# Attention and a SwiGLU block in one kernel: key rests of four heads in one score unit, a written-out order for batch 0, loads ordered by need

## The chip, the cores and the metric

The kernel runs on one core of a Trainium2 chip. The metric is the device time of one execution, in microseconds. Before the change the median of three runs is 453.41 us (453.38 to 453.52). The profile is of one execution whose instructions span 451.7 us.

In the profile PE is TensorE (PEld its weight loads), ACT is ScalarE, DVE is VectorE, POOL is GpSimd and SP is SyncE, which here only issues DMA. A "chunk" or "unit" in this text is one PSUM tile of scores with the one exponential that reads it.

## What is computed

Eight batches of twelve heads, 448 positions, head size 64. Softmax attention, heads put side by side into rows of 768, then a gated FFN with 1536 inner columns:

```python
scores = q @ k.T / sqrt(64)                 # per batch and head, 448 x 448
attn   = softmax(scores)                    # over keys
x      = (attn @ v) -> [8*448, 768]         # heads side by side
g      = x @ w_gate                         # [3584, 1536]
out    = (g * sigmoid(g) * (x @ w_val)) @ w_out     # [3584, 768], float32
```

## The kernel before

Matmuls run in FP16 with FP32 accumulation. Two heads make a pair: 48 pairs, six per batch. Scores are computed transposed, keys on partitions, so that the exponentials can be the stationary operand of the product with V. A column of ones beside V gives the sum of the exponentials, and the division comes at the end, on 128 queries at a time.

The 448 keys of a pair are cut into four chunks of 112. A chunk is two matmuls (one for each head, on the upper and the lower 64 rows of the array) and one exponential over 896 columns:

```python
def qk(pr, c):
    t = qkT[pr]
    s = ps_s.tile([128, 2, 512], FP32, tag="s")          # ring of 3, two banks each
    for hx in range(2):
        nc.tensor.matmul(s[:, hx, 0:S],
            lhsT=t[ts(hx, 64), c * P : c * P + 128],     # P = 112 keys
            rhs=t[ts(hx, 64), ds(S + (1 - hx) * D, S)], start=True, stop=True)
    e = Es[pr % NE][:, ds(c * EB, 16)].rearrange("p (h b) x -> p h (b x)", h=2)
    nc.scalar.activation(e[:, :, 0:S], s[0:P, :, 0:S], AF.Exp, scale=sm_scale)
```

The product with V (PV) takes 448 queries as three groups of 128 for each head; the remaining 64 queries of both heads share a seventh group, so that one accumulator of one PSUM bank holds a pair:

```python
def pv_chunk(pr, c):
    if c == 0:
        accs[pr] = ps_f.tile([128, 512], FP32, tag="f", name="acc")   # ring of 2 banks
    ...
    for j in range(3):
        for hx in range(2):
            nc.tensor.matmul(a7[:, 2 * j + hx], lhsT=e[...], rhs=vo[:, hx, c, 0 : D + 1], ...)
    for hx in range(2):
        nc.tensor.matmul(a7[:, 6], lhsT=e[...], rhs=vo[:, hx, c, 0 : D + 1], ...)
    ...                                # after the last chunk: reciprocal, multiply, into xt
```

That makes 8 matmuls of 65 columns a chunk and 32 a pair. The result must be turned (`turn_x`) to be the moving operand of the FFN. For pairs below XPE = 12 PE does it, with the rests of a batch turned together in `turn_rests`; from there on two DMA transposes do it. q and k are turned by PE below pair NPE = 11 (18 transposes of 112 columns a pair) and by DMA after that.

The FFN works in eight blocks of 384 and 512 tokens by turns. Each has 12 steps of gate and value (six matmuls each), and two output groups of 12 matmuls for each 128 tokens:

```python
gp = ps_f.tile(...) if gate_small[0] else ps_s.tile([128, 2, 512], FP32, tag="s")[:, 0]
group("g", gp)                                  # 6 matmuls
nc.scalar.activation(sg, gp, AF.Tanh, scale=0.5)
vp = ps_f.tile([128, 512], FP32, tag="f")
group("v", vp)                                  # 6 matmuls
... t = (sg + 1) * gp ; hts = t * vp            # both on DVE
```

The output of a chunk of 128 tokens is written at the end of its second half. The very last chunk is treated apart: its halves go out singly, and the second half in two pieces of 192 columns.

```python
last = last_block and ch == n // 128 - 1
...
parts = [(oh * OH, OH)]
if last and oh:
    parts = [(OH, OH // 2), (OH + OH // 2, OH // 2)]
```

The program has a start, in which the attention of batch 0 (pairs 0 to 5) is done as a loop over 24 chunks with PV, transposes and loads placed between them, and a main loop of "visits". A visit issues two or three chunks of scores, up to two PVs of earlier pairs, and a share of the FFN's steps. Loads are issued by GpSimd, which also turns FP32 into FP16 in the DMA; the lists `wq` say at which pair each load is issued.

Of the kernel before, what the change touches and what calls it, by code (L numbers as in the profile page):

```python
# [10 lines left out]
FP32 = mybir.dt.float32  # L11
# [6 lines left out]
NB = 2  # L18
GP = 3
NPE = 11  # L20
# [3 lines left out]
WIDE = 8  # L24
XPE = 12
NE = 4
NX = 6
NV = 5
VS = 9
EB = 15  # L30
# [3 lines left out]
def kernel(  # L34
# [24 lines left out]
    MQ = S - D  # L59
# [13 lines left out]
    load_table("exp_and_others")  # L73

# [7 lines left out]
    ps_f = ctx.enter_context(tc.tile_pool(name="ps_f", bufs=2, space=PSUM))  # L82

    Es = [consts.tile([P, NC * EB + 1, D], FP16, name=f"E{i}") for i in range(NE)]
    Xts = [consts.tile([128, 7, D], FP16, name=f"xt{i}") for i in range(NX)]
    Xrs = [consts.tile([D, 128], FP16, name=f"xr{i}") for i in range(3)]
    Vts = [consts.tile([P, 2, NC, D + 2], FP16, name=f"vo{i}") for i in range(NV)]
    vraw = consts.tile([P, VS, 2, NC, D], FP16, name="vraw")
# [11 lines left out]
    wo = [consts.tile([128, NFB, OH], FP16, name=f"wo{i}") for i in range(2)]  # L100
# [5 lines left out]
    def dummy(n):  # L106
        wp = ps_f.tile([128, 512], FP32, tag="f", name="wp")
        for _ in range(n):
            nc.tensor.matmul(wp[:], lhsT=warm[:, 0:128], rhs=warm[:], start=True, stop=True)  # L109

    def load_qk32(pr):
        rq = raws.tile([P, 2, NC, D], FP32, tag="rq", bufs=RB)
        rk = raws.tile([P, 2, NC, D], FP32, tag="rk", bufs=RB)
        for dst, src in ((rq, q), (rk, k)):
            nc.sync.dma_start(dst[:], src[0, 2 * pr : 2 * pr + 2].rearrange("h (p c) d -> p h (c d)", c=NC))
        raw[pr] = (rq[:], rk[:])
# [3 lines left out]
    def load_qk16(pr, n=2):  # L120
        h0 = 2 * (pr % 2) if pr >= 14 else 0
        if h0 == 0:
            q16 = raws.tile([P, 4, NC, D], FP16, tag="rq", bufs=RB, name="q16")
            k16 = raws.tile([P, 4, NC, D], FP16, tag="rk", bufs=RB, name="k16")
            pairbuf[:] = [q16, k16]
        q16, k16 = pairbuf
        for dst, src in ((q16, q), (k16, k)):
            flat = src.rearrange("b h s d -> (b h) s d")[2 * pr : 2 * pr + 2 * n]
            nc.gpsimd.dma_start(dst[:, ds(h0, 2 * n)], flat.rearrange("h (p c) d -> p h (c d)", c=NC))  # L129
        for i in range(n):  # L130
            h = h0 + 2 * i
            raw[pr + i] = (q16[:, h : h + 2], k16[:, h : h + 2])

    def load_v(pr, n=1):
        b, h = divmod(2 * pr, H)
        nc.gpsimd.dma_start(  # L136
            vraw[:, ds(pr % VS, n)].rearrange("p r h c d -> p (r h) (c d)"),
            v[b, h : h + 2 * n].rearrange("h (p c) d -> p h (c d)", c=NC),
        )
# [4 lines left out]
    def load_w(kind, i):  # L144
        if kind == "o":
            src = moe_w_out[:, ts(i, OH)].rearrange("(f p) m -> p f m", p=128)
            dst = wo[i]
        else:
            src = (moe_w_gate if kind == "g" else moe_w_val)[:, ts(i, DF // 4)].rearrange(
                "(t a p) m -> t p a m", p=128, t=2  # L150
            )
            for t in range(2):
                nc.gpsimd.dma_start(wgv[kind, i][:, ts(t, NCB // 2), :], src[t])
            return
        nc.gpsimd.dma_start(dst[:], src)

    def prep(pr):
        rq, rk = raw[pr]
        if pr == 0 or pr >= NPE:
            qk16 = attp.tile([P, 2, NC, 2, D], FP16, tag="qk16", bufs=3)  # L160
            for t, src in enumerate((rq, rk)):
                dst = qk16[:, 1 - t].rearrange("p c h d -> p h c d")
                if pr == 0:
                    nc.vector.tensor_copy(dst[:, 0], src[:, 0])
                    nc.scalar.activation(dst[:, 1], src[:, 1], AF.Copy)
                else:
                    nc.gpsimd.tensor_copy(dst, src)  # L167
        qkT[pr] = attp.tile([128, 2 * S + D], FP16, tag="qkT", name="qkT", bufs=5)
        if pr >= NPE:
            nc.sync.dma_start_transpose(  # L170
                qkT[pr][:, 0 : 2 * S].rearrange("p (c q) -> p c q", q=P),
                qk16[:].rearrange("p t c h d -> p (t c h d)"),
            )
            nc.sync.dma_start_transpose(
                qkT[pr][:, 2 * S :].rearrange("p (c q) -> p c q", c=1),
                qk16[0:D, 1, 0].rearrange("p h d -> p (h d)"),
            )
            return None

        def turn0():  # L180
            for t in range(2):
                tp = ps_s.tile([128, 2, 512], FP32, tag="s", name="tp")
                for c in range(NC):
                    for hx in range(2):
                        nc.tensor.matmul(
                            tp[ts(hx, 64), c // 2, ds(c % 2 * P, P)],
                            lhsT=qk16[:, 1 - t, c, hx],
                            rhs=ident[0:P, 0:P],
                            start=True,
                            stop=True,  # L190
                        )
                dst = qkT[pr][:, ts(1 - t, S)].rearrange("p (a x) -> p a x", a=2)
                nc.vector.tensor_copy(dst[:, 0], tp[:, 0, 0 : 2 * P])
                nc.scalar.activation(dst[:, 1], tp[:, 1, 0 : 2 * P], AF.Copy)
                if t == 0:
                    tq = tp
            nc.vector.tensor_copy(qkT[pr][:, 2 * S :], tq[:, 0, 0:D])

        def turn():
            if pr < FIRST + 2:  # L200
                tp = ps_s.tile([128, 2, 1024], FP16, tag="s", name="tp")[:, 0]
            else:
                tp = ps_f.tile([128, 1024], FP16, tag="f", name="tp")
            for i in range(2 * NC + 1):
                t, c = (1 - i // NC, i % NC) if i < 2 * NC else (0, 0)
                for hx in range(2):
                    src = raw[pr][t][:, hx, c, :]
                    nc.tensor.transpose(tp[ts(hx, 64), ts(i, P)], src, ident[0:P, 0:P])  # L208
            nc.vector.tensor_copy(qkT[pr][:], tp[:, 0 : 2 * S + D])  # L209
# [3 lines left out]
    def qk(pr, c):  # L213
        t = qkT[pr]
        s = ps_s.tile([128, 2, 512], FP32, tag="s")
        for hx in range(2):
            nc.tensor.matmul(  # L217
                s[:, hx, 0:S],
                lhsT=t[ts(hx, 64), c * P : c * P + 128],
                rhs=t[ts(hx, 64), ds(S + (1 - hx) * D, S)],  # L220
                start=True,
                stop=True,
            )
        e = Es[pr % NE][:, ds(c * EB, 16)].rearrange("p (h b) x -> p h (b x)", h=2)
        nc.scalar.activation(e[:, :, 0:S], s[0:P, :, 0:S], AF.Exp, scale=sm_scale)  # L225

    def qk_half(pr, half, between=None):
        for c in (2 * half, 2 * half + 1):
            qk(pr, c)
            if between and c % 2 == 0:  # L230
                between()
# [3 lines left out]
    def pv_chunk(pr, c):  # L235
        if c == 0:
            accs[pr] = ps_f.tile([128, 512], FP32, tag="f", name="acc")
        e = Es[pr % NE]
        vo = Vts[pr % NV]
        a7 = accs[pr][:, 0 : 7 * (D + 1)].rearrange("p (s d) -> p s d", s=7)  # L240
        for j in range(3):
            for hx in range(2):
                nc.tensor.matmul(  # L243
                    a7[:, 2 * j + hx],
                    lhsT=e[:, ds(c * EB + 9 * hx + 2 * j, 2)].rearrange("p b x -> p (b x)"),
                    rhs=vo[:, hx, c, 0 : D + 1],
                    start=c + j + hx == 0,
                    stop=False,
                )
        for hx in range(2):  # L250
            nc.tensor.matmul(  # L251
                a7[:, 6],
                lhsT=e[:, ds(c * EB + 6 + hx, 2)].rearrange("p b x -> p (b x)"),
                rhs=vo[:, hx, c, 0 : D + 1],
                start=False,
                stop=c == NC - 1 and hx == 1,
            )
        if c < NC - 1:
            return
        r = attp.tile([128, 8], FP32, tag="R", bufs=2, name="R")  # L260
        xt = Xts[pr % NX]
        nc.vector.reciprocal(r[:, 0:7], a7[:, :, D])  # L262
        n = 7 if pr < XPE else 6
        nc.vector.tensor_tensor(  # L264
            xt[:, 0:n],
            a7[:, 0:n, 0:D],
            r[:, 0:n].unsqueeze(2).to_broadcast([128, n, D]),
            ALU.mult,
        )
        if pr < XPE:  # L270
            return
# [370 lines left out]
```

The softmax here doesn't subtract the row's maximum and nothing guards it: scores larger than these inputs give would overflow.

## Time and profile before

| what | value |
|---|---|
| median time | 453.41 us |
| span of the profiled execution | 451.7 us |
| exponentials (ACT, L225) | 192, 919 ns each |
| PV matmuls (PE, L243 and L251) | 1536 |
| first gate matmul of the FFN | 29.95 us |
| last matmul ends | about 446.6 us |
| granted TensorE clock | 0.998 |

A row of groups reads: line, engine, operation, output and inputs, shape, count, then the busy time and mean ns of one, then the idle time of the engine before them and what ended it. A row of waits reads: who waited for what, the total in us, how many times, and the longest. The chain of waits follows the work that ended last back to the start; a row in order of time has its start, its length and its kind. A row of the timeline has a start, a length, engine, line and operation, and in square brackets the idle time ahead of it.

The page gives busy shares by fortieths of the span. PE is at nine tenths from the second slice to the last but one. ACT is at 9 tenths in the second, and between 4 and 7 through most of the rest until the last pairs are done.

### The profile page before, as it was taken

To read this page: it belongs to the slowest core of one execution; us is meant where nothing else is said; L and a number is where in the kernel's file an instruction comes from. 1 tells how busy PE (TensorE), PEld (TensorE's weight loads), DVE (VectorE), ACT (ScalarE), POOL (GpSimd) and SP (SyncE) were. 2 spreads that over 40 slices of the span, in tenths; PEclk is the share of its full clock that TensorE was granted. 3 is DMA by queue.
4 is the path that set the end of the run, shared out by engine and by line. 5 is a ranking of instruction groups with operands and counts; after the bars stand their busy time and mean duration, and the time that the engine had idled before them with its cause. 6 is when DMAs were issued, how large, how long until landed. Compare 5 with 4: busy or idle time off the path is not lost.

```text
span 451.7 us, 9871 instructions
## 1 busy us (share of the span) xinstructions
PE 441.9 (98%) x4024; PEld 247.0 (55%) x4024; DVE 201.6 (45%) x447; ACT 238.8 (53%) x350; POOL 141.8 (31%) x228
## 2 busy tenths in 40 slices
PE   8999999999999999999999999999999999999995
PEld 3655565545455556454555656545455666544563
DVE  3666562456654434455443534353453544055300
ACT  6965666566746465554554546644555462222221
POOL 8755715927642225252313405330100000000000
PEclk9999999999999999999999999999999999999999
DMA  9999999999969379874749758772503112200033
GB/s 142 173 200 201 196 172 174 180 209 119 145 93 133 46 129 124 132 120 71 126 74 120 98 78 143 118 105 68 101 20 68 46 46 57 70 2 0 17 100 95
DMA packets 105101, 48.71 MB, mean 108 GB/s; under 512 B 59744, under 2 KB 101600, under 8 KB 105056
## 3 DMA queue, kind: packets, MB, share of 16 engines
q0 software_dynamic: 43392, 23.37, 41.2%
q1 hardware_dynamic: 61664, 24.71, 28.9%
q8 instruction: 31, 0.51, 0.5%
q14 instruction: 14, 0.11, 0.1%
HBM read 47.19 MB, written 11.01 MB: 129 GB/s over the span
## 4 chain that ended last, share of the span: by engine, by line
PE 93%; DVE 3%; ACT 2%; issue 1%; DVEq 0%; ACTq 0%
PE op L371 24%; PE gp L326 23%; PE vp L326 23%; PE s L217 9%; PE acc L243 9%; PE acc L251 2%; ACT E L225 2%; PE tp L208 1%; PE wp L109 1%; DVE t L345 1%; ACT sg L341 1%; DVE qkT L209 0%; DVE xt L264 0%; PE acc L291 0%; DVE hts L348 0%
## 5 line engine op out<-in xcount | busy, mean ns | idle before, releaser
L225 ACT ACTIVATE E<-s 112x896 f16<-112x896 f32 x192 | 162.1, 919 | 27.5 <-PE s L217 27.4
L326 PE MATMUL gp<-X,wg 128*128 128x384 f16 (+1 forms) x576 | 124.7, 352 | 0.0
L326 PE MATMUL vp<-X,wv 128*128 128x384 f16 (+1 forms) x576 | 124.6, 352 | 0.0
L371 PE MATMUL op<-wo,hts 128*128 128x384 f16 (+1 forms) x684 | 116.1, 323 | 0.0
L345 DVE SCALAR_TENSOR_TENSOR t<-sg,gp 128x384 f32<-128x384 f32 (+1 forms) x96 | 59.7, 621 | 121.8 <-ACT sg L341 121.8
L341 ACT ACTIVATE sg<-gp 128x384 f32<-128x384 f32 (+1 forms) x96 | 52.5, 547 | 84.8 <-PE gp L326 83.6
L371 PEld LDWEIGHTS <-hts 128*128 128x128 f16 x684 | 65.5, 98 | 45.9 <-issue 3.9
L326 PEld LDWEIGHTS <-wv 128*128 128x128 f16 x576 | 56.3, 98 | 52.6
L326 PEld LDWEIGHTS <-wg 128*128 128x128 f16 x576 | 53.1, 97 | 45.6 <-issue 1.1
L378 ACT ACTIVATE osb<-op 128x384 f32<-128x384 f32 (+1 forms) x57 | 27.8, 487 | 92.5 <-PE op L371 92.5
L167 POOL COPY qk<-q 112x512 f16<-112x512 f16 x37 | 22.9, 619 | 144.5 <-DMA qkT<-qk 143.1
L348 DVE SCALAR_TENSOR_TENSOR hts<-t,vp 128x384 f16<-128x384 f32 (+1 forms) x96 | 59.6, 621 | 10.0
L243 PEld LDWEIGHTS <-E 112*128 112x128 f16 x1152 | 46.7, 97 | 18.2 <-issue 17.5
L243 PE MATMUL acc<-vo,E 112*128 112x65 f16 x1152 | 53.0, 193 | 1.3 <-DVE vo L142 0.7
L217 PE MATMUL s<-qkT 64*128 64x448 f16 x384 | 50.6, 355 | 0.2
L251 PE MATMUL acc<-vo,E 112*128 112x65 f16 x384 | 42.9, 193 | 0.0
L262 DVE RECIPROCAL R<-acc 128x7 f32<-128x7 f32 x48 | 9.8, 205 | 70.6 <-PE acc L251 70.5
L129 POOL DMA_DIRECT2D k<-in_k_dram x44 | 29.0, 660 | 9.5 <-DMA wo<-in_moe_w_out_dram 7.8
L129 POOL DMA_DIRECT2D q<-in_q_dram x44 | 29.3, 666 | 5.2 <-PE s L217 2.5
L136 POOL DMA_DIRECT2D vraw<-in_v_dram x42 | 28.0, 666 | 8.4 <-DVE vo L142 7.2
L217 PEld LDWEIGHTS <-qkT 64*128 64x128 f16 x384 | 14.5, 94 | 25.8 <-issue 18.6
L264 DVE TENSOR_TENSOR xt<-acc,R 128x384 f16<-128x384 f32 (+1 forms) x48 | 27.6, 574 | 1.7
(41 smaller groups left out, 148.2 us busy)
## 6 DMA issues: line engine op xcount, KB each, us to landing
q<-in_q_dram POOLq DMA_DIRECT2D x41, 112.0 KB, 4.0
k<-in_k_dram POOLq DMA_DIRECT2D x41, 112.0 KB, 4.6
vraw<-in_v_dram POOLq DMA_DIRECT2D x39, 112.0 KB, 4.6
wg<-in_moe_w_gate_dram POOLq DMA_DIRECT2D x8, 288.0 KB, 10.1
wv<-in_moe_w_val_dram POOLq DMA_DIRECT2D x8, 288.0 KB, 10.2
wo<-in_moe_w_out_dram POOLq DMA_DIRECT2D x2, 1152.0 KB, 22.0
out_dram<-osb SPq DMA_DIRECT2D x8, 288.0 KB, 3.0
out_dram<-osb SPq DMA_DIRECT2D x8, 240.0 KB, 3.1
```

Source lines behind the costliest of these rows:

```text
L129: nc.gpsimd.dma_start(dst[:, ds(h0, 2 * n)], flat.rearrange("h (p c) d -> p h (c d)", c=NC))
L136: nc.gpsimd.dma_start(vraw[:, ds(pr % VS, n)].rearrange("p r h c d -> p (r h) (c d)"), v[b, h : h + 2 * n].rearrange("h (p c) d -> p h (c ...
L217: nc.tensor.matmul(s[:, hx, 0:S], lhsT=t[ts(hx, 64), c * P : c * P + 128], rhs=t[ts(hx, 64), ds(S + (1 - hx) * D, S)], start=True, stop=True,)
L225: nc.scalar.activation(e[:, :, 0:S], s[0:P, :, 0:S], AF.Exp, scale=sm_scale)
L243: nc.tensor.matmul(a7[:, 2 * j + hx], lhsT=e[:, ds(c * EB + 9 * hx + 2 * j, 2)].rearrange("p b x -> p (b x)"), rhs=vo[:, hx, c, 0 : D + 1] ...
L251: nc.tensor.matmul(a7[:, 6], lhsT=e[:, ds(c * EB + 6 + hx, 2)].rearrange("p b x -> p (b x)"), rhs=vo[:, hx, c, 0 : D + 1], start=False, st ...
L326: nc.tensor.matmul(dst[:, 0:n], lhsT=wslice(kind, fb, cb), rhs=X[kk][:, cb, ds(c0, n)], start=(cb == 0), stop=(cb == NCB - 1),)
L341: nc.scalar.activation(sg[:, 0:n], gp[:, 0:n], AF.Tanh, scale=0.5)
L345: nc.vector.scalar_tensor_tensor(t1[:, 0:n], sg[:, 0:n], 1.0, gp[:, 0:n], ALU.add, ALU.mult)
L348: nc.vector.scalar_tensor_tensor(hts[:, fb, 0:n], t1[:, 0:n], 0.5 * HS, vp[:, 0:n], ALU.mult, ALU.mult)
L371: nc.tensor.matmul(op[:, 0:w], lhsT=hts[:, fb, ts(ch, 128)], rhs=wo[oh][:, fb, ds(m0 - oh * OH, w)], start=(fb == 0), stop=(fb == NFB - 1),)
L378: nc.scalar.activation(osb[:, ds(m0, w)], op[:, 0:w], AF.Copy, scale=1.0 / HS)
```

## The change

It has five parts.

1. **Key rests shared by four heads.** The keys of a head are now three chunks of 128 and a rest of 64. The rests of both heads of two neighbouring pairs make one unit: four matmuls of 64 x 64 on the four quadrants of the array, into one tile, and one exponential. Two pairs take 7 exponentials in place of 8. Whether a head's rest is its first or its last keys depends on pair and head (`low`), so that PV of the rest uses the half of the rows on which it lies.
2. **PV with an accumulator for each head.** A head has four groups of queries (the fourth with 64 used ones) in a bank of its own, so a pair takes two banks. A pair still has 32 matmuls, 8 of them on 64 rows. In the start there is one accumulator of two banks, from a pool of its own; after it these banks are the f ring.
3. **Other layouts.** q and k of pairs 0 to 11 are loaded with 7 rows of 64 values in each of 64 partitions per head, and turned by PE in 30 transposes of 64 columns. Keys and values of the later pairs (values of all) are loaded by two DMAs of 64 partitions each, 8/7 as many bytes.
4. **Batch 0 in a written-out order.** A string says in which order score units (s), transposes (t), copies of V (v), pieces of PV (p) and X (x) are issued. It holds 23 score units: the 21 of batch 0 and two of pair 6.
5. **Loads and other placement.** Pair 9 is loaded ahead of the second pair of weight slices, pairs 10 and 11 and V of pairs 9 to 11 ahead of the third. `w_out` is loaded in four pieces at pairs 9 and 10. X of batch 2 (pairs 12 to 17) is turned by PE, and all X of batches 0 to 2 with its rests at once. Pair 0 is loaded by two queues. A visit has three units and at most one PV, and the FFN's steps are dealt out over the visits anew.

The core of the diff, with cuts:

```diff
-NPE = 11
+NPE = 12
-WIDE = 8
-XPE = 12
+XPE = 18
-NX = 6
+NX = 3
+START = (
+    "sstssvtsppsppstvsxsvpspppstsppsppsvtsspp"
+    "pvxspsxspppvpstsppxsppsxx"
+)
...
     def load_qk32(pr):
-        for dst, src in ((rq, q), (rk, k)):
-            nc.sync.dma_start(dst[:], src[0, 2 * pr : 2 * pr + 2].rearrange("h (p c) d -> p h (c d)", c=NC))
+        nc.sync.dma_start(rk[:], halves(k, 2 * pr, 1)[:, 0])
+        nc.scalar.dma_start(rq[:], halves(q, 2 * pr, 1)[:, 0])
...
     def qk(pr, c):
+        if c < KR:                                   # KR = 3 units of 128 keys
+            ...
+        else:
+            for hx in range(2):
+                for p in (pr, pr + 1):
+                    lo = low(p, hx)
+                    t = qkT[p]
+                    nc.tensor.matmul(
+                        s[ts(1 - lo, 64), hx, 0:S],
+                        lhsT=t[ts(hx, 64), ds(0 if lo else KR * 128 + 64, 64)],
+                        rhs=t[ts(hx, 64), ds(NC * 128, S)],
+                        start=True,
+                        stop=True,
+                    )
+            e = Ers[pr // 2 % NR][:]
+        nc.scalar.activation(
+            e[:, 0 : 2 * S].rearrange("p (h q) -> p h q", h=2), s[:, :, 0:S], AF.Exp, scale=sm_scale
+        )
...
+    def pv_open(pr):
+        if pr not in accs:
+            if pr < FIRST:
+                acc = psum["a"].tile([128, 2, 512], FP32, tag="a", name="acc")
+                accs[pr] = ([acc[:, 0], acc[:, 1]], [0, 0], acc)
+            else:
+                accs[pr] = ([fbank(), fbank()], [0, 0])
...
     def ffn2_steps(kk, c0, n, hts, first, last_block):
...
                 while l < l0 + 128:
                     b, j = divmod(l, S)
-                    c, p0 = divmod((j + D) % S, P)
-                    m = min(P - p0, l0 + 128 - l, (MQ if j < MQ else S) - j)
+                    n = S // groups(kk)
+                    c, p0 = divmod(j, n)
+                    m = min(n - p0, l0 + 128 - l)
...
         wq = {
             0: [("qk", 6), ("g", 0), ("v", 0)],
-            1: [("V", 2), ("qk", 8, 1), ("g", 1), ("v", 1)],
-            3: [("qk", 9, 1), ("qk", 10), ("g", 2), ("v", 2)],
-            4: [("g", 3), ("v", 3), ("qk", 12)],
-            6: [("V", 3), ("o", 0)],
-            7: [("o", 1)],
+            1: [("V", 2), ("qk", 8, 1), ("qk", 9, 1), ("g", 1), ("v", 1)],
+            3: [("qk", 10), ("V", 3), ("g", 2), ("v", 2)],
+            4: [("qk", 12), ("g", 3), ("v", 3)],
+            9: [("o", 0), ("o", 1)],
+            10: [("o", 2), ("o", 3)],
         }
...
-            n = 2 if g < WIDE * NC else 3
+            n = 2 if g == NU0 else 3
-            while queue and queue[0][0] <= g and len(todo) < 2:
+            while queue and queue[0][0] <= g and len(todo) < 1:
...
+                for pr, c in sorted(chunks, key=lambda x: -(x[1] == RU)):
+                    qk(pr, c)
+                for _, p0 in todo:
+                    pv_piece(p0, RU)
```

## The prediction

> **What bounds the kernel now.** I read four views in this order: busy time, the waits of PE, the chain of waits cut into stretches, and the timeline of the first 30 us. Busy time first, then the whole list of what PE waits for:
>
> ```profile
> PE 441.9 (98%) x4024; PEld 247.0 (55%) x4024; DVE 201.6 (45%) x447; ACT 238.8 (53%) x350; POOL 141.8 (31%) x228
> ```
> ```profile
> PE wp L109 <- DVE warm L407: 1.2, 1, 1.2
> PE acc L291 <- DVE xt L264: 1.0, 1, 1.0
> PE acc L243 <- DVE vo L142: 0.7, 1, 0.7
> PE acc L243 <- DVE t L345: 0.4, 1, 0.4
> PE rtp L310 <- ACT osb L378: 0.4, 1, 0.4
> PE tp L208 <- DVE hts L348: 0.2, 1, 0.2
> PE rtp L310 <- DVE t L345: 0.2, 1, 0.2
> ```
>
> PE is busy for 98% and its listed waits (columns: us in total, times, longest) add up to 4.1 us. A busy PE can still hide gaps, since matmul records overlap, so I take prices from starts in the chain of waits (start, us, what):
>
> ```profile
> 84.82 0.67 PE s L217 x6
> 85.49 0.29 PE acc L243 x6
> 85.78 0.06 PE acc L251 x2
> 85.84 0.18 PE acc L243 x6
> 86.02 0.06 PE acc L251 x2
> ...
> 86.56 1.30 PE gp L326 x6
> ...
> 382.29 1.95 PE op L371 x12
> ```
>
> A visit of the main loop is three score units (0.67 us for six matmuls), one pair's PV (32 matmuls, 84.82+0.67 to 86.56: 1.07 us), and FFN work. Twelve op matmuls take 1.95 us, six gate ones of 512 columns 1.30 (of 384 columns 0.98). So FFN alone is 48 x 2 x 0.975 + 48 x 2 x 1.295 = 217.9 us for gate and value, and 55 x 1.95 + 24 x 0.08 = 109.3 us for the output. That is 327 of the span's 451.7 us, and the change does not touch it.
>
> The first 30 us are different. The timeline of ACT:
>
> ```profile
> 6.59 5.04 ACT L225 ACTIVATE E<-s 112x896 f16<-112x896 f32 x6 [0.42 <-PE s L217]
> 13.57 6.65 ACT L225 ACTIVATE E<-s 112x896 f16<-112x896 f32 x8
> 23.25 6.08 ACT L225 ACTIVATE E<-s 112x896 f16<-112x896 f32 x7 [0.29 <-PE s L217]
> ```
>
> The exponentials run one after another, 0.84 us apart (5.04/6), with under 1 us of gaps from 6.59 to 29.33; the first gate matmul starts at 29.95. Here ACT sets the end. Later it does not.
>
> **What the Trainium skill says.** "ScalarE: Activation LUTs", What ACT_TABLE_LOAD costs: an ACTIVATE with immediate scale and bias takes 186 ns + 0.833 ns per element, and neighbours overlap by about 93 ns. For 896 elements: 932 and 839 ns. The trace agrees (919 mean, 840 apart), and partitions do not enter, so 128 rows of keys in place of 112 are free. "TensorE: Matmul & The Clock Gate", Back-to-back issue gap: N/2.4 + 2.5 ns; 384 columns give 162.5 ns, the trace 1.95/12 = 162.5. "TensorEngine Tiling (Array Packing)", Key Properties: different tiles run in parallel, and changing the tiling mode drains the array. The trace agrees with both: six score matmuls (two row halves) take three slots of 0.19 us plus 0.10; eighteen transposes of 112 columns (two column halves) take 0.57 us, nine slots and a drain. No run yet shows four quadrants at once.
>
> **The change, part by part.** 1. *Exponentials.* 192 become 144 + 24 = 168. In the main loop ACT has slack, so this is worth time only at the start.
>
> 2. *Scores, main loop.* After the FFN begins, 166 chunks remain now (pairs 6 to 47, less two issued before it); then 124 plain units and 21 shared ones, again less two. I count a shared unit, four 64x64 matmuls on four quadrants, as one slot of 0.19 us. Slots: 166 x 0.19 = 31.5 us now, 145 x 0.19 = 27.6 then: **-3.9**. Drains: 57 visits with scores now (three of two chunks, the others of three), 49 then, two drains of about 0.1 each, and 21 more for the quadrant mode: 11.4 against 11.9: **+0.5**.
>
> 3. *PV.* Still 32 matmuls a pair at 0.030 us (0.24 for 8). Eight of them now use half the rows, the two heads on opposite halves, so I count them as four slots: 28 slots for 32, -0.12 us, x 42 pairs: **-5.0**. PV of the rest follows the scores in the same tiling mode, so no drain is added.
>
> 4. *q/k transposes.* 30 of 64 columns in place of 18 of 112, in 15 slots of 0.03: about 0.57 us as now. But five pairs (7 to 11) fall into the main loop where three did: **+1.2**.
>
> 5. *X on PE.* Twelve pairs at about 0.3 us, where now six at 0.26 and two collected rests at 0.38: **+1.0**. The DMA transposes of batch 2 disappear; nothing on PE waits for them now, so that gains nothing I can see.
>
> 6. *The start.* 23 exponentials before the FFN where 26 stand now: 3 x 0.84 = **-2.5** us, with the first at about 6.6 as now. FFN should begin near 27.4. Loading pair 0 by two queues in parallel saves at most 0.3, which I leave for the larger memsets and 30 start transposes. The start has a single accumulator, emptied by DVE in about 1 us after each pair, but its order puts two to six other items between the last PV piece of a pair and the first of the next.
>
> 7. *New waits.* PV opens two accumulators, one per head, and the f ring has two banks, so it needs both free when a visit begins. Output eviction is 0.49 us and scores come first (0.67), so after an output group no wait. After a value group hts ends some 0.75 us later (ACT and DVE rows), a wait of 0.1 or so. In the first visits the shared unit goes first and needs the keys of a pair turned just before (pairs 7 and 9): up to 1 us each. I book **+2.2**; most of today's roughly 2 us of waits in the main loop remain.
>
> 8. *The end.* In the changed ffn2_steps the loop over output pieces assigns n = S // groups(kk). That overwrites the block's n, so `last` is never true: the final chunk is no longer cut, and goes out as 16x768 and 112x768 after its last half. Now the last eviction is 0.33 us (192 columns), then 0.49; now the last pieces are of 48 KB, landing in 2.0 us by the DMA rows, then one of 336 KB (4.2 with traffic beside it, perhaps 3.0 alone). 0.16 + about 1.1: **+1.3**.
>
> Sum: -3.9 + 0.5 - 5.0 + 1.2 + 1.0 - 2.5 + 2.2 + 1.3 = -5.2 us; 453.4 - 5.2 = 448.2. I write **448.0**.
>
> **The rivals.** *A: half-size matmuls do not overlap.* If weight loads or issue keep the four quadrants and the half-row PV apart, the -5.0 goes, the shared units cost 21 x 0.19 = 4 us more and five transpositions about 0.45 each: some 459 us. For it: PV slots are only 0.03 us and need a 128-column weight load each. Against it: twelve rtp matmuls of 64 columns take 0.31 us from start to start with a drain, about half of what twelve single slots (0.36) plus a drain would need. *B: the two accumulators become the bound.* A wait of 0.4 us in each of 42 visits adds 17 us: about 463. Against it, DVE needs roughly 0.65 us per head (reciprocal 0.2, multiply about 0.45 by its 0.56 for 384 columns), and the first value group needs its bank only after a gate group of 0.98 us or more. *C: ACT was a bound in the main loop too.* The chain's list has 7.3 us of ACT E, 2.9 of sg and 3.7 of DVE t, much of it between 30 and 120 us. If that were all PE idle time, 24 fewer exponentials would save some 10 us more: 438. Against it, PE's own waits total 0.4 us for DVE t and none for ACT E: the chain passes through ACT there though PE had work. *D: data come late.* V loads are doubled in number and 8/7 as long, and V of pairs 13 and 14 now queues behind the 4.7 MB of wo, which at the 200 GB/s of slices 3 to 8 is 24 us. A late V would stop DVE, then PE, for one to four us: 450 to 452. In favour of the change, q/k of the first twelve pairs come in 1792-byte rows where 1024-byte ones came.
>
> **Range and chances.** Parts 2 and 3 rest on overlaps that the trace shows only in similar forms: half of them failing costs 5 us. Waits are uncertain by 2 to 3 us, the start by 1.5, the end by 1. Together about 5 us each way: 443.5 to 453.5. The 2% lines are 444.3 and 462.5. Beyond the first needs C or a start that gains twice what I count; beyond the second needs A or B in full. I give 0.15 for faster, 0.81 for within 2%, 0.04 for slower.
>
> **What would show it.** Part 6: first gate matmul at 27 to 28 us, 23 exponentials before it. Parts 2 and 3: in a late visit the four matmuls of a shared unit about 0.3 us with its drain, eight PV matmuls of the rest in 0.12 us, a whole PV in about 0.95. Part 4: 0.57 us from the first of 30 transposes to what follows. Part 7: PE's waits for DVE hts, t, qkT or R between 27 and 80 us, together 2 to 4 us. Part 8: from the last matmul to the end of the span 5.1 us now, 6.4 then. The prediction is wrong if the rests' PV takes 0.24 us, if PE waits for vo or the accumulators in most visits, or if the FFN starts after 29 us.

## The result, and the profile after

The changed kernel takes 464.11 us (median of 4 runs, 463.46 to 465.47) where the kernel before, beside it on the same chip, took 453.47 (453.38 to 453.80). The ratio is 1.0237, 95% interval 1.0213 to 1.0261: **slower by 2.4%**, 16 us above the predicted 448.0 and outside its range.

First the page of the kernel after: busy time, and in fortieths of the span (11.5 us each) PE and its granted clock in tenths.

```profile
PE 438.5 (95%) x4184; PEld 247.7 (54%) x4184; DVE 203.6 (44%) x466; ACT 219.3 (48%) x325; POOL 180.8 (39%) x303
...
PE   7898869999999999999999999999999999999995
...
PEclk9999998999999999999999999999999999999999
```

PE has 3.4 us less work than before (438.5 against 441.9) in a span 9.8 us longer. The work did shrink; the time went into slices 4 to 6, from 35 to 70 us, where PE is at 8 and 6 tenths, and the next slice has the clock at 8. Before, nothing fell below 9 there. So I ask what PE waits for between 27 and 135 us (columns: us in total, times, longest):

```profile
PE s L265 <- DMA qkT<-qk: 3.5, 1, 3.5
PE s L252 <- DVE qkT L243: 2.6, 3, 1.2
PE s L265 <- DVE qkT L243: 1.6, 2, 1.0
PE f L423 <- DVE hts L400: 1.4, 2, 0.7
PE f L287 <- DVE hts L400: 1.1, 4, 0.5
PE s L252 <- DMA qkT<-qk: 0.8, 1, 0.8
PE f L287 <- DVE t L397: 0.4, 1, 0.4
PE xtp L354 <- issue: 0.3, 1, 0.3
```

That is 11.7 us of listed waits (the last row, 0.3, lies just ahead of the first FFN block), where the kernel before has some 1.2 in its first two FFN blocks. At the head stand scores that wait for q and k turned by DMA, a wait that the kernel before does not have at all, and scores that wait until DVE has copied q and k turned by PE.

The starts of the first gate matmul of each FFN block, from PE's timeline, say how much each stretch is worth. (The 29.95 us given further up for the kernel before is where the chain of waits counts this matmul from; in the timeline it begins at 29.79.) In blocks 0 and 1 both kernels do the same FFN work (144 gate, 144 value and 72 output matmuls) and the PV of 14 pairs; in blocks 2 to 6 the same FFN work again and the PV of 28 pairs.

| stretch | before, us | after, us | difference |
|---|---|---|---|
| start, to the first gate matmul | 29.8 | 27.8 | -2.0 |
| blocks 0 and 1 | 100.1 | 113.9 | **+13.9** |
| blocks 2 to 6 | 264.0 | 262.3 | -1.6 |
| block 7 | 52.7 | 52.7 | 0 |
| last matmul to the end of the span | 5.2 | 4.7 | -0.4 |

The whole loss lies in blocks 0 and 1. Here is the long wait in the timeline of the kernel after (start, us, engine, operation; the idle time ahead of it in brackets):

```profile
57.98 1.46 SPq L200 DMA_TRANSPOSE qkT<-qk  x1
...
59.49 1.29 SPq L204 DMA_TRANSPOSE qkT<-qk  x1
...
64.24 0.37 PE L265 MATMUL s<-qkT 64*64 64x448 f16 x1
...
68.15 0.38 PE L265 MATMUL s<-qkT 64*64 64x448 f16 x3 [3.54 <-DMA qkT<-qk]
...
68.57 0.92 ACT L273 ACTIVATE er<-s 128x896 f16<-128x896 f32 x1 [4.91 <-PE s L265]
```

The shared unit of pairs 12 and 13 begins at 64.24, finds pair 13 not yet turned, and holds all of PE until 68.15. The transpose that it needs was issued at 59.49, 8.7 us before. The kernel before issues its transposes of pair 13 at nearly the same time:

```profile
56.65 3.69 SPq L170 DMA_TRANSPOSE qkT<-qk  x1
60.38 1.22 SPq L174 DMA_TRANSPOSE qkT<-qk  x1
```

But it scores pair 13 some 10 us later, as shown below. Are transposes slower after the change? The DMA issues of 45 to 70 us (count, then median us from issue to landing), before and after, and after over the whole program:

```profile
qkT<-qk SPq DMA_TRANSPOSE x6, 11.1
```
```profile
qkT<-qk SPq DMA_TRANSPOSE x7, 8.6
```
```profile
qkT<-qk SPq DMA_TRANSPOSE x72, 4.2
```

They are not: in that stretch, in which the queues carry 185 GB/s before and 193 after, they take two to three times their usual time, and before the change even longer. **The data come no later; they are asked for earlier.** Counted in score units, pair 12 is first scored in the visit that begins at 71.72 before the change, pair 13 in the one at 74.45:

```profile
71.72 0.74 PE L217 MATMUL s<-qkT 64*128 64x448 f16 x6
...
74.45 0.74 PE L217 MATMUL s<-qkT 64*128 64x448 f16 x6
```

After, the visit of pair 12 begins at 59.23 and that of pair 13 at 64.24:

```profile
59.23 0.74 PE L252 MATMUL s<-qkT 64*128 64x448 f16 x6
```

Block 0 begins 2 us sooner after the change, and by the first score of pair 12 PE has done seven steps of gate and value (13.7 us), where it had done twelve and two output groups (27.3 us). The six output groups of block 0 (11.7 us) are in block 1 now, which leaves less FFN work for each visit; and with three units in every visit pair 12 comes in the eighth visit, not in the tenth. No run takes these two apart. Together they bring the attention of batch 2 forward by 10 to 12 us, while the loads keep their place.

The idle time has a second price. Windows (PE, PEld, DVE, ACT, POOL busy, then granted clock, DMA share, GB/s) of before, then of after:

```profile
60.00:80.00 20.00, 19.57 (x229) 12.15 (x227) 8.81 (x21) 13.28 (x19) 7.88 (x13) 1.00 1.30 168
```
```profile
60.00:80.00 20.00, 14.84 (x167) 9.58 (x167) 9.61 (x26) 9.21 (x13) 13.30 (x23) 0.91 1.27 190
```

A mean clock of 0.91 over 20 us is 1.8 us of full speed lost. A finer window of the kernel after shows where:

```profile
68.82:72.20 3.38, 3.38 (x42) 2.37 (x37) 1.21 (x4) 2.29 (x3) 2.71 (x5) 0.50 1.16 202
```

The clock is at half for 3.4 us, which costs 1.7 us. Six gate matmuls of 384 columns just after the wait take 1.79 us, from 70.56 to 72.35, where they take 0.98 elsewhere. "TensorE: Matmul & The Clock Gate" in the Trainium skill, Part 1, says that the clock falls to half after an idle window of about 3.4 us and comes back after about as long of work. This trace agrees: 3.5 us idle, then half the clock for 3.4 us. A later run does not fit the first figure: there a wait of 2.8 us was enough.

### The profile page after: what moved, and what is told of

It reads as the page before. It is cut to its first block, busy times and chain, and to the rows that moved or that the text cites. A ratio compares the mean times of both kernels' runs of the same rounds, so it can differ in the third digit from the quotient of the medians.

```text
span 461.5 us, 10232 instructions
## 1 busy us (share of the span) xinstructions
PE 438.5 (95%) x4184; PEld 247.7 (54%) x4184; DVE 203.6 (44%) x466; ACT 219.3 (48%) x325; POOL 180.8 (39%) x303
## 4 chain that ended last, share of the span: by engine, by line
PE 82%; DMA 5%; ACT 4%; DVE 4%; POOL 2%; issue 1%; SPq 0%; DVEq 0%; ACTq 0%
PE f L423 24%; PE f L378 21%; PE gp L378 20%; PE f L287 8%; PE s L252 5%; DMA qkT<-qk 3%; ACT E L273 2%; DMA q<-in_q_dram 2%; DVE hts L400 2%; DVE t L397 2%; ACT sg L393 1%; PE s L265 1%; DMA rk<-in_k_dram 1%; PE acc L287 1%; POOL qk L196 1%
## 5 line engine op out<-in xcount | busy, mean ns | idle before, releaser
L273 ACT ACTIVATE E<-s 128x896 f16<-128x896 f32 x144 | 123.0, 923 | 13.8 <-PE s L252 13.8
L378 PE MATMUL f<-X,wv 128*128 128x384 f16 (+1 forms) x576 | 124.6, 352 | 0.0
L423 PE MATMUL f<-wo,hts 128*128 128x384 f16 x672 | 115.5, 326 | 1.4 <-DVE hts L400 1.4
L378 PE MATMUL gp<-X,wg 128*128 128x512 f16 (+1 forms) x522 | 114.3, 355 | 0.0
L430 ACT ACTIVATE osb<-f 128x384 f32<-128x384 f32 x56 | 27.5, 491 | 109.1 <-PE f L423 102.5
L196 POOL COPY qk<-k 128x512 f16<-128x512 f16 x36 | 23.3, 647 | 118.5 <-DMA qkT<-qk 118.5
L400 DVE SCALAR_TENSOR_TENSOR hts<-t,f 128x384 f16<-128x384 f32 (+1 forms) x96 | 59.6, 621 | 10.0
L287 PEld LDWEIGHTS <-E 128*128 128x128 f16 x1152 | 38.4, 98 | 4.0 <-issue 1.2
L287 PE MATMUL f<-vo,E 128*128 128x65 f16 x1008 | 38.6, 195 | 0.0
L326 DVE TENSOR_TENSOR xt<-f,R 128x256 f16<-128x256 f32 x84 | 35.6, 424 | 3.1 <-DVE R L325 0.3
```

Source lines behind the costliest of these rows:

```text
L196: nc.gpsimd.tensor_copy(dst.rearrange("p c h d -> p h c d"), src)
L273: nc.scalar.activation(e[:, 0 : 2 * S].rearrange("p (h q) -> p h q", h=2), s[:, :, 0:S], AF.Exp, scale=sm_scale)
L287: nc.tensor.matmul(accs[pr][0][hx][:, ts(j, D + 1)], lhsT=e[rows, ds(hx * S + j * 128, 128)], rhs=Vts[pr % NV][rows, hx, col, 0 : D + 1], ...
L326: nc.vector.tensor_tensor(xt[:, :, hx], a4[:, :, 0:D], r[:].unsqueeze(2).to_broadcast([128, KR + 1, D]), ALU.mult,)
L378: nc.tensor.matmul(dst[:, 0:n], lhsT=wslice(kind, fb, cb), rhs=X[kk][:, cb, ds(c0, n)], start=(cb == 0), stop=(cb == NCB - 1),)
L400: nc.vector.scalar_tensor_tensor(hts[:, fb, 0:n], t1[:, 0:n], 0.5 * HS, vp[:, 0:n], ALU.mult, ALU.mult)
```

## The experiments

Two theories at first. **D**: PE waits for q and k of pairs 13 (3.5 us) and 14 (0.8 us) because their transposes come late out of DMA queues full of weights, above all `w_out`. **T**: PE waits because the PE transposes of pairs 7 to 11 stand at the end of a visit, just ahead of the scores that need them, and DVE must copy them in between. Both can be true; the runs price them. Each run has the kernel before beside it on the same chip, at a median of 453.2 to 453.7 us. Its ratio to that is given with the 95% interval; differences between experiments are differences of medians.

### PE transposes ahead of the gate group

```diff
-                later.append(x + 7)
+                prep(x + 7)()
```

> Change: the 30 transposes of pairs 7 to 11 are issued right after PV and ahead of the visit's first gate group, not after the first gate and value group; the rest as in the changed kernel (464.1 us). Theory O (order: the scores follow the transposes so closely that DVE's copy of qkT is on the path): PE's waits for DVE qkT between 30 and 53 us, together about 5 us, go; about 459. Theory D (data: the first pairs turned by DMA are late, whatever PE does before): the 5 us come back as a longer wait for DMA qkT near 64 us; 463 to 464, with that wait at 8 us or so in place of 3.5.

Measured: 465.12 us, ratio 1.0265 (1.0224 to 1.0306), no better than the changed kernel. T's waits are gone from the list of 27 to 135 us, and D's have grown:

```profile
PE s L265 <- DMA qkT<-qk: 3.4, 1, 3.4
PE s L252 <- DMA qkT<-qk: 2.2, 1, 2.2
```

The clock is 0.67 from 60 to 70 us and 0.82 from 70 to 80, about 5 us of full speed. PE comes sooner to the pairs whose data it must then wait for. T's 4.2 us are real, but cannot be cashed while D stands. The reason given for them holds for three of the five visits (at 30.57, 35.01 and 40.68, 2.8 us). In the other two (46.50 and 51.74, 1.4 us) the waiting unit belongs to a pair turned a visit earlier; there the copy has to free a tile of the score ring, which has three.

### `w_out` at pairs 13 and 14

```diff
-            9: [("o", 0), ("o", 1)],
-            10: [("o", 2), ("o", 3)],
+            13: [("o", 0), ("o", 1)],
+            14: [("o", 2), ("o", 3)],
```

> Change: the four pieces of the output weights are issued at pairs 13 and 14 in place of 9 and 10; the rest as in the changed kernel (464.1 us). Theory D (4.7 MB of output weights stand in the queues ahead of, and beside, the turning of pairs 12 and 13): PE's waits for DMA qkT (3.5 + 0.8 us) and the slow clock after them (about 1.5 us) go; about 458. Theory O: those waits come from the late issue by GpSimd, which works through its list in order, and not from the weights; less than 2 us are won, 462 to 464. If the weights are then late for the output groups, a wait of PE for wo near 100 us shows it.

Measured: 457.61 us, ratio 1.0085 (1.0062 to 1.0109). This alone returns 6.5 us (block 0 is 5.7 us shorter in the profile), close to what the two DMA waits (4.3) and the clock (1.7) add up to. PE's waits, at their head:

```profile
PE s L252 <- DVE qkT L243: 2.6, 3, 1.2
PE s L265 <- DVE qkT L243: 1.6, 2, 1.0
```

No DMA stands in the list any more, T's rows are unchanged to the tenth, and the clock is 1.00 throughout. Pair 13 is turned at 55.70 and 56.94 and scored at 63.83 without a wait.

The rival named in that text, the late issue by GpSimd, is about half of how the weights do harm. GpSimd also makes the copies that the transposes read, in the order of its list. In the changed kernel two pieces of `w_out` stand ahead of the copies of pair 13; with late `w_out` the copies begin 2.3 us sooner (GpSimd's timeline, the changed kernel and then this one):

```profile
56.57 0.76 POOL L176 DMA_DIRECT2D wo<-in_moe_w_out_dram  x1 [0.28 <-DMA k<-in_k_dram]
57.33 0.62 POOL L196 COPY qk<-k 128x512 f16<-128x512 f16 x1
```
```profile
55.05 0.62 POOL L196 COPY qk<-k 128x512 f16<-128x512 f16 x1
```

The transposes themselves then take 5.0 and 5.9 us to land in place of 8.6. No run moves one of the two without the other.

### `w_out` earlier still, at pairs 6 and 7

The opposite edit, in the changed kernel:

```diff
-            9: [("o", 0), ("o", 1)],
-            10: [("o", 2), ("o", 3)],
+            6: [("o", 0), ("o", 1)],
+            7: [("o", 2), ("o", 3)],
```

> Change: in the changed kernel (464.1 us) the four pieces of the output weights are issued at pairs 6 and 7, where the kernel before issues them (at 45.9 us, with no wait of PE for DMA qkT). Theory D in its final form: the loss is not the place of these loads in itself but that place against a main loop which, without output groups in block 0, reaches pairs 12 and 13 at 57 and 64 us in place of some 72 and 80 us; with the 4.7 MB wholly ahead of their transposes the wait for DMA qkT grows from 4.3 us to 8 to 12 us: 468 to 473. Rival: what counts is that the output weights are out of the queues before the transposes are issued, as in the kernel before; then the waits shrink, and the time is 460 or less.

(Two of the times in this text are off: the changed kernel reaches pair 12 in the visit at 59.23, and the kernel before reaches pair 13 in the one at 74.45.) Measured: 467.99 us, ratio 1.0317 (1.0300 to 1.0334), 3.9 us slower than the changed kernel. PE's longest wait, and the window of 60 to 80 us:

```profile
PE s L252 <- DMA qkT<-qk: 9.1, 1, 9.1
```
```profile
60.00:80.00 20.00, 11.83 (x120) 7.50 (x120) 6.60 (x18) 5.62 (x8) 13.87 (x24) 0.74 1.33 158
```

One wait of 9.1 us, for pair 12, ended at 67.70, and 5 us of clock. Moving the same 4.7 MB both ways moves the wait both ways: D is shown, not only argued. It also supports the earlier need as the cause: here the last transpose of pair 12 lands 11.8 us after its issue at 55.74; the kernel before, with `w_out` at the same pairs, has it landed 10.8 us after its issue at 55.05, only 1.7 us sooner, and does not wait, because it scores the pair some 13 us later.

### Both edits

> Change: both edits, transposes ahead of the gate group and output weights at pairs 13 and 14. If the two losses are separate and each as large as its waits, about 464.1 - 5 - 6 = 453. If DMA is the limit of the first 70 us in itself (about 200 GB/s, with all loads of twelve pairs and the weights to move), only one of the two gains is had: 457 to 459.

Measured: 457.57 us, ratio 1.0079 (1.0051 to 1.0108), the same as with late `w_out` alone. T's rows are gone, and a DMA wait of 2.2 us for pair 12 has come back, ended at 59.02: its transposes were issued at 49.13 and 50.50. Again PE ran into the data. Unlike in the changed kernel, the clock stayed at 1.00 after this 2.2 us in the profiled execution.

### PV of the rests head by head

A test of rival A of the prediction. If half-row matmuls overlap only with a neighbour on the other half of the rows, four of one head and then four of the other should take twice as long.

```diff
+        if c == RU:
+            for hx in heads:
+                for j in range(KR + 1):
+                    pv_mm(pr, hx, c, j)
+            return
```

> Change: the eight matmuls of PV on the rests are issued head by head (four on one half of the rows, then four on the other), not alternating; the same work. If the halves overlap only when neighbours lie on different halves, as the prediction assumed, eight take 0.24 us and not 0.12: 0.12 x 48 pairs = some 5 us more, 469. If they don't overlap in either order, or overlap in both, 464.

Measured: 464.49 us, ratio 1.0234 (1.0211 to 1.0258), no difference. PE's timeline in the start, eight PV matmuls of the rests and the scores that follow in the same tiling mode, of the changed kernel and then of this one:

```profile
11.05 0.29 PE L287 MATMUL acc<-vo,er 64*128 64x65 f16 x8
11.19 0.35 PE L252 MATMUL s<-qkT 64*128 64x448 f16 x2
```
```profile
11.02 0.30 PE L287 MATMUL acc<-vo,er 64*128 64x65 f16 x8
11.15 0.36 PE L252 MATMUL s<-qkT 64*128 64x448 f16 x2
```

0.14 and 0.13 us for eight, about half of the 0.24 us that eight full ones take. Blocks 2 to 6 agree: 262.5 us with this edit, 262.3 without, where twice the time would add 0.12 for each of 28 pairs, 3.4 us. The halves overlap in both orders, and rival A is not the cause.

### X turned in the score ring

X of pairs 6 to 17 takes a bank of the f ring, beside accumulators, value groups and output groups. It goes to the ring of scores instead, on top of early transposes and late `w_out`:

```diff
-            if pr < FIRST:
-                tp = ps_s.tile([128, 2, 512], FP32, tag="s", name="xtp")[:, 0]
-            else:
-                tp = fbank()
+            tp = ps_s.tile([128, 2, 512], FP32, tag="s", name="xtp")[:, 0]
```

> Base: transposes ahead of the gate group and output weights at pairs 13 and 14 (457.6 us in the earlier run). Change: X of pairs 6 to 17 is turned by PE in a tile of the score ring and no longer in one of the two f banks. Theory F (two accumulators use up both f banks, so a third user of them costs waits): PE's waits for DVE X (1.4 us), the two 0.7 us waits of output groups for hts and a part of the 0.2 to 0.5 us waits of PV on the rests go; about 454. Rival: the waits are set by DVE's queue and not by the bank; PV or the scores wait elsewhere instead, 457 to 458.

Measured: 455.63 us, ratio 1.0050 (1.0038 to 1.0062), 1.9 us better; block 1, in which no run waits for DMA, is 55.9 us long in place of 57.7. The waits of the output groups for hts (1.4 us) are gone, and five new ones have come, of scores for the copy of X:

```profile
PE s L252 <- DVE X L358: 3.1, 5, 0.7
```

The wait has partly moved from one ring to the other.

### The last chunk cut again

On top of that, the local name in `ffn2_steps` is changed, so that the block's `n` survives and `last` comes true:

```diff
-                    n = S // groups(kk)
+                    ng = S // groups(kk)
```

(with the two uses of it)

> Base: as the run with X in the score ring. Change: the count in the output loop has a name of its own, so that the last chunk of 128 tokens is again cut in pieces (the halves apart, the second half in two of 192 columns). As the prediction had it, 1.3 us faster than without the cut. As the traces have it (5.1 us from the last matmul to the end before, 4.7 after), no gain, or some 0.4 us slower.

Measured: 454.47 us, ratio 1.0029 (1.0017 to 1.0041), 1.2 us better, though the intervals of the two ratios overlap. In the profiles the last matmul ends at the same place (448.7 in both), and the time after it is 3.8 us in place of 4.7. So the overwritten name cost 0.9 to 1.2 us; the prediction said 1.3.

### Gate and value slices 3 later

On top of the cut last chunk:

```diff
-            4: [("qk", 12), ("g", 3), ("v", 3)],
+            4: [("qk", 12)],
+            9: [("g", 3), ("v", 3)],
```

> Base: as the run with the last chunk cut. Change: the last pair of weight slices (gate and value, 2.4 MB) is issued at pair 9, behind the turning of pair 12, and not at pair 4. Theory D: the remaining wait for DMA qkT of pair 12 (2.2 us near 57 us) goes, 2 us faster. Against it: the slices are needed for the tenth step of block 0, near 60 us; if they land too late, PE waits for wg instead and nothing is won, or the time rises by up to 5 us.

Measured: 458.75 us, ratio 1.0109 (1.0093 to 1.0124), a miss. Pair 12 came in time; the weights, now at the place where `w_out` had been, took the queue ahead of pair 13, which waited 3.6 us, up to 66.9. In this run as with `w_out`, what lies ahead of the pair that is needed next sets the wait, whichever bytes they are.

### X of batch 2 by DMA again

On top of early transposes and late `w_out`:

```diff
-XPE = 18
+XPE = 12
```

> Base: transposes ahead of the gate group and output weights at pairs 13 and 14 (457.6 us). Change: X of batch 2 (pairs 12 to 17) is turned by DMA again, as in the kernel before, so this part of the change is undone alone. If turning it on PE only costs: six times about 0.25 us of PE and the two waits of 0.7 us for hts go, 454.5. If DMA is so full up to 110 us that these transposes come late or delay those of q and k, it is no faster, or slower: 457 to 460 with PE waiting for DMA X or DMA qkT.

Measured: 455.10 us, ratio 1.0038 (1.0026 to 1.0051), 2.5 us better than both edits alone. The profile is of its slowest execution (457.32 us), with a DMA wait of 2.8 us and a clock of 0.69 from 60 to 70 us; block 1, past all that, is 54.9 us long in place of 57.7. Turning X of batch 2 on PE is a loss in this kernel; the score ring alone returned 1.7 us of these 2.7.

### X between the gate and the value group

On top of the cut last chunk: the visit's X is turned while ACT works on the gate group.

```diff
             nc.scalar.activation(sg[:, 0:n], gp[:, 0:n], AF.Tanh, scale=0.5)
+            while mid:
+                turn_x(mid.pop(0))
             vp = fbank()
...
-                    turns.append(p0)
+                    mid.append(p0)
```

> Base: the run with X in the score ring and the last chunk cut (454.5 us), in which the third score unit of five visits of block 0 waits 0.6 to 0.7 us for DVE's copy of X, 3.1 us in all. Change: X is turned between the first gate and value group of a visit, not after the value group, so that DVE copies it ahead of hts. Theory F: 3 us go, and so do the 0.2 us waits of PV on the rests that follow; 451.5. Theory D: the next transposes by DMA are needed 3 us earlier and their wait grows by as much (1.3 to about 4 us near 57 us); 454.5 and no gain.

Measured: 454.57 us, ratio 1.0021 (1.0010 to 1.0031), nothing gained. The waits for X are gone and D is back:

```profile
PE s L252 <- DMA qkT<-qk: 3.5, 1, 3.5
```

It is the third time that time won ahead of pair 12 turns into a wait at pair 12.

### Pair 12 ahead of the weights

On top of that, pairs 12 and 13 loaded before the third weight slices, the fourth at pair 8, and transposes issued four pairs ahead:

```diff
-            3: [("qk", 10), ("V", 3), ("g", 2), ("v", 2)],
-            4: [("qk", 12), ("g", 3), ("v", 3)],
+            3: [("qk", 10), ("V", 3), ("qk", 12), ("g", 2), ("v", 2)],
+            8: [("g", 3), ("v", 3)],
...
-                if NPE <= pr + 3 < NPAIR:
-                    prep(pr + 3)
+                if NPE <= pr + 4 < NPAIR:
+                    prep(pr + 4)
```

> Base: as the run with X between gate and value group. Change: q and k of pairs 12 and 13 are loaded ahead of the third pair of weight slices, the pairs turned by DMA are turned one pair earlier (four ahead in place of three), and the last pair of weight slices is issued at pair 8, behind that. Theory D: PE's waits for DMA qkT go and the gains of the order add up: 450 to 451, faster than the kernel before (453.3). If GpSimd, which works through its list in order, now stands waiting for loads, weights come late and PE waits for wg near 60 us: 453 to 456.

Measured: 453.14 us, ratio 0.9994 (0.9984 to 1.0003): level with the kernel before, 2 to 3 us short of what was hoped for. SP's timeline, pairs 12 and 13:

```profile
43.08 1.31 SPq L200 DMA_TRANSPOSE qkT<-qk  x1
44.45 1.25 SPq L204 DMA_TRANSPOSE qkT<-qk  x1
49.08 1.19 SPq L200 DMA_TRANSPOSE qkT<-qk  x1
50.32 1.25 SPq L204 DMA_TRANSPOSE qkT<-qk  x1
```

Six and nine us sooner than in the changed kernel. The transposes of 45 to 70 us take 7.7 us to land (median), little less than the 8.6 of the changed kernel, and PE does not wait for them.

### And X of batch 2 by DMA

The same edit of XPE on top of the last kernel:

```diff
-XPE = 18
+XPE = 12
```

> Base: as the run with pairs 12 and 13 ahead. Change: X of batch 2 by DMA again. Block 1 was 1.0 us shorter with it in the run that undid this part (54.9 against 56.0 us with X in the score ring). If nothing else moves, 1 us faster, 449 to 450; if the transposes then delay q and k, no gain.

Measured: **451.46 us** (450.66 to 452.43, 6 runs), ratio **0.9954 (0.9940 to 0.9969)**: faster than both kernels, by 0.5% of the kernel before. PE's busy share:

```profile
PE 438.0 (97%) x4172; PEld 246.8 (55%) x4172; DVE 199.7 (44%) x460; ACT 220.1 (49%) x326; POOL 180.9 (40%) x303
```

PE works the same 438 us as in the changed kernel, 11.8 us of span sooner (449.7 against 461.5).

## Why the prediction was wrong

**The step that failed is part 7, new waits, +2.2.** The excess over it lies in blocks 0 and 1. There the prediction's own terms give, for 14 of the 42 pairs, (-3.9 + 0.5 - 5.0)/3 = -2.8, and +1.2, +1.0 and +2.2: +1.6 us in all. Measured was +13.9. The listed waits in these blocks are 11.4 us less 1.2 before, and the lost clock 1.7: 11.9 us stand where 2.2 were booked. The sum is then -2.8 + 1.2 + 1.0 + 11.9 = 11.3, and 2.6 us of the 13.9 stay without a row; a part of them is what parts 2 and 3 promised too much, below.

It failed in three places. It did not ask **when** each pair would be needed: dealing out the FFN's steps anew, without output groups in block 0, changes no sum, and it brings the attention of batch 2 forward by 10 to 12 us. Rival D had the right queue and the right 4.7 MB, but named V, and at one to four us; it was the transposed q and k that came late, 4.3 us of waits, and the 1.7 us of clock that follow a long idle time were not in it (6.5 us together, by late `w_out`). Part 7 gave the transposes of pairs 7 and 9 up to 1 us each; it was all five, 4.2 us. And part 5 counted X on PE by its matmuls alone, though X is one more user of the f ring: output groups then waited 1.4 us for hts.

The other points:

- *Part 6, the start*: right in kind. First gate matmul at 27.8 (27 to 28 predicted, from 29.79 and not 29.95), 23 exponentials ahead of it, the first at 6.93 instead of 6.6. It gave -2.0, not -2.5.
- *Part 2 and rival A*: the four quadrants do work at once. In the visit at 56 us of the kernel after, the shared unit begins 0.32 us ahead of the next unit, drain included, as predicted ("about 0.3"):

```profile
56.37 0.38 PE L265 MATMUL s<-qkT 64*64 64x448 f16 x4
...
56.69 0.55 PE L252 MATMUL s<-qkT 64*128 64x448 f16 x4
```

- *Part 3*: eight half-row matmuls take 0.13 to 0.14 us, as predicted (0.12). But I took the whole PV of before as 1.07 us from a chain; in the timeline it runs from 66.60 to 67.56, 0.96 us. After, in later visits, PV of the rest takes 0.28 us with the drain and small waits, and the 24 full ones 0.74. A visit's three scores and a PV went from 0.68 + 0.96 = 1.64 us to 0.58 + 0.28 + 0.74 = 1.60, or, with a shared unit among the three, 0.71 + 0.21 + 0.74 = 1.66 (the visit at 229.76).
- *Parts 2 and 3 together were too large*: 28/42 of -8.4 is -5.6 us for blocks 2 to 6. Measured was -1.6. PE's listed waits there, none before, took back 1.4: PV for hts (1.0) and for an output copy (0.4). With the 1.5 us that PV waits for hts and t in blocks 0 and 1 this is rival B, at a sixth of the 17 us that it named. Most of the rest is the visit itself, 0.04 us shorter where part 3 promised 0.12: for 28 pairs an estimated 2.2 us.
- *Part 4*: right. Thirty transposes from 34.42 to the scores at 35.01, 0.59 us against 0.57.
- *Part 8*: right in kind and wrong in sum. The missing cut costs 0.9 to 1.2 us, as the run with its own name shows, but the end became 0.4 us shorter and not 1.3 longer. In the kernel before, the last pieces are issued by SP one after another, and SP ends 1.95 us after the last eviction (446.92 to 448.87); after, 0.81 (457.30 to 458.11). I had compared landing times alone.
- *Rival C*: fell. Blocks 2 to 6, with 15 exponentials fewer, gained 1.6 us.
- Two small slips change nothing: 55 x 1.95 + 24 x 0.08 is 109.2 and not 109.3, and the listed waits of the kernel before in the main loop are 1.2 us and not roughly 2.

The best version of these experiments, with most waits gone and X by DMA, took 451.46 us and not 448.0. It has the same 262.3 us in blocks 2 to 6 as the changed kernel, so the 4 us that parts 2 and 3 promised there too much are still missing. No experiment takes them apart.

## What to carry to other kernels

When work leaves a stage that runs beside full DMA queues, list for each transfer when it lands and when it is first needed, before and after: the sum of the work does not show that a need has moved ahead of its data. While one late transfer stands, every gain made ahead of it turns into a longer wait at it (early transposes with and without late `w_out`, and X between gate and value, show that), so the order of the loads comes first and the waits on engines after it. And in these runs each wait of 2.8 us or more cost more than itself, because the clock fell behind it.

## What the runs showed of the hardware

The lost clock comes in steps. Summed over the ten-microsecond windows from 50 to 80 us, as 10 us times one minus the granted clock, it is 1.7 us in the changed kernel (longest wait 3.5), 1.7 with the slices 3 late (3.6) and 1.8 with X between gate and value (3.5); 3.4 with `XPE = 12` on both edits (2.8) and 3.4 in the head-by-head run (4.5); about 5.2 with the early transposes (3.4 and 2.2) and 5.1 with `w_out` early (9.1). It is nothing after the wait of 2.2 with both edits. So it is about one, two or three times 1.7 us, which fits a clock at half for stretches of 3.4 us: the window of 68.82 to 72.20 in the changed kernel has a clock of 0.50, and so has that of 59.50 to 66.20 with `XPE = 12` on both edits. The number of stretches does not follow from the length of the longest wait alone. Half-row matmuls overlap whether their halves alternate or come in two blocks of four: 0.14 and 0.13 us for eight of 65 columns.

GpSimd, which issues the loads, makes the copies for the transposes in the same order of instructions, so they can be late with the loads: in the run with `w_out` at pairs 6 and 7 it stands idle for 1.9 and 2.5 us ahead of two loads of V, until a piece of `w_out` has landed by the profile, and only then comes to the copies of pair 13, at 67.92 and not at 57.33 as in the changed kernel.
